# Attention slots taken in pairs once the feed-forward products of the mixer are interleaved with them

## The chip, the cores and the metric

One Trainium2 chip, one NeuronCore. The metric is device time in microseconds (us) of one execution. Before the change it is 1092.57 us, the median of three executions (1092.56, 1092.57 and 1092.97). The profiled execution has a span of 1089.3 us.

## What is computed

Two stages in a row, all in fp32 on 4 batches, 768 positions and 512 channels:

```python
# attention, per batch and head (8 heads of width 64)
scores = where(block_mask, q @ k.T / 8, -1e9)     # blocks of 32: window, first, last, 3 random
x = softmax(scores) @ v                            # heads side by side: (4, 768, 512)
# mixer
u = x + real(fft(fft(x, axis=1), axis=2))
un = (u - mean(u)) / sqrt(var(u) + 1e-6)
out = u + relu(un @ w_ch1) @ w_ch2                 # 512 -> 2048 -> 512
```

## The kernel before

**The unit.** Attention works on pairs of heads (index `n`, 16 in all, four for each batch). A *unit* is one block of 128 keys against 384 queries (half of the 768) for the two heads of a pair. There are 12 units for each head pair: 6 key blocks (`c`) for each of two halves. A unit is made of four pieces:

- `scores` (line 536): the two heads' products k·q, four matrix instructions at line 551. Each head uses 64 rows of the array, so that two run side by side. The result is a PSUM tile `s` of two banks; the pool `ps_s` (line 182) has two of them.
- `weigh` (line 563): ScalarE takes the exponential of `s` in place (line 572), VectorE multiplies it by the mask into an SBUF tile `e` (line 574; the pool `ep`, line 174, has four), and GpSimd adds `e` into a running sum `acc` (line 584). The tile `s` is free when VectorE has read it. (In the first batch the mask is put in by a product, and ScalarE writes `e` itself.)
- `values` (line 587): the two heads' products with v, four matrix instructions at line 597, each head on 64 columns of the array. They accumulate over the 6 key blocks in the single PSUM tile `o` (line 183). After the sixth, `o` is copied out as `oT`, by VectorE (line 604) or ScalarE (line 607), and the next half can write `o`.
- once for each half, `place` or `place_blocks` puts `oT` into the mixer's input `x` (the latter by 16 DMA transfers, line 635), and once for each head pair `total` sums `acc` by TensorE (line 677).

**The mixer.** Its "rest" for a batch is a list of `channel` steps: eight `quad` steps (line 979; seven products of 1.3 us in the plan's figures, a first-layer block with ReLU) and 24 `channels` steps (line 1044; 3.45 us, eight instructions at line 1048, then an add into `x` by VectorE at line 1051). They stand in the order quad, quad, six `channels`, four times. A quad borrows both `s` tiles (line 1009) from its third product on. All that comes ahead of it in the mixer (Fourier sums, normalisation, transposes) is a list of `apart` steps.

**The order.** It is written out by the host when the program is built. `slot(sl)` (line 1271) is called for `sl` = 0 to 96; a slot has two units, six slots make a head pair (`s` = 0 to 5), 24 a batch (`r` = 0 to 23). A slot issues, in this order: the scores of its two units, their `weigh`, the `values` of the *previous* slot's units, loads, then channel steps, then `short` steps (transposes, `place`, `total`). How many channel steps is set by a debt: `state["owed"]` grows by `pace` in each slot and a step is issued as soon as half of it is owed (lines 1332 to 1340). `pace` spreads what is in `late` beyond `COVER` (100 us) over the slots that are left of the batch, and is at least 2.5 us. `gap` (line 1215), called ahead of and after each channel step, slips in `apart` steps that are ready by the host's own estimates.

At two points of a batch (`s` = 5 of its first head pair and `s` = 1 of its second, lines 1298 and 1313) `until` issues all channel steps of the batch two before, since the memory of its `x` is needed. Channels of the first batch are all issued there, so only slots 54 to 96 have any beside them. `BY_VECTOR` = 9: from head pair 9 on, q and k are turned by VectorE (`flip_blocks`, line 514) and put in order by ScalarE (`in_order`, line 523), not by TensorE.

Of the kernel before, what the change touches and what calls it, by code (L numbers as in the profile page):

```python
# [102 lines left out]
def kernel(  # L103
# [16 lines left out]
    B, H, S, D = q.shape  # L120
# [12 lines left out]
    T = C // 2  # L133
# [58 lines left out]
    def busy(engine, us, after=0.0):  # L192
        when[engine] = max(when[engine], after) + us
        return when[engine]
# [13 lines left out]
    pairs = [(b, j) for b in range(B) for j in range(NP)]  # L208
# [325 lines left out]
    SLOT = 2  # L534

    def scores(us):

        n, w = divmod(us[0], UP)
        half = w // C
        qT, kT = turned[n, 0], turned[n, 1]  # L540
        queries = slice(half * HS, (half + 1) * HS)
        got = []
        for u in us:
            c = u % C
            s = ps_s.tile([P, 2, 512], FP32, tag="s", name="s")
            got.append((u, s))
            busy("PE", 0.72, max(e_at.get(u - SLOT, 0.0), z_at[u % 2]))
            s_at[u] = when["PE"] + HOP
            for i in range(2):
                rows = slice(D * i, D * i + D)  # L550
                nc.tensor.matmul(s[:, i, 0:HS], kT[rows, c * P:(c + 1) * P], qT[rows, queries],  # L551
                                 start=True, stop=n >= NP)
        for u, s in got if n < NP else ():
            c = u % C
            busy("PE", 0.25)
            s_at[u] = when["PE"] + HOP
            for i in range(2):
                rows = slice(D * i, D * i + D)
                nc.tensor.matmul(s[:, i, 0:HS], of_k[rows, c * P:(c + 1) * P], off_q[rows, queries],
                                 start=False, stop=True)  # L560
        return got

    def weigh(u, s):
        n, w = divmod(u, UP)
        half, c = divmod(w, C)
        e = ep.tile([P, 2, HS], FP32, tag="e", name="e")
        e_of[u] = e
        if n < NP:
            nc.scalar.activation(out=e, in_=s[:, :, 0:HS], func=ACT.Exp, scale=scale)
            e_at[u] = busy("ACT", 0.8, s_at[u]) + HOP  # L570
            return
        nc.scalar.activation(out=s[:, :, 0:HS], in_=s[:, :, 0:HS], func=ACT.Exp, scale=scale)  # L572
        m = mask[:, c, half * HS:(half + 1) * HS].rearrange("p (o s) -> p o s", o=1)
        nc.vector.tensor_tensor(out=e, in0=s[:, :, 0:HS], in1=m.broadcast_to([P, 2, HS]),  # L574
                                op=ALU.mult)
        e_at[u] = busy("DVE", 0.97, busy("ACT", 0.8, s_at[u]) + HOP) + HOP
        if c > 0:
            acc_at[n, half] = busy("POOL", 2.0, e_at[u]) + HOP
        if c == 1:
            acc_of[n, half] = acc_p.tile([P, 2, HS], FP32, tag="acc", name="acc")  # L580

        for i in range(2 if c > 0 else 0):
            acc = acc_of[n, half][:, i, :]
            nc.gpsimd.tensor_add(out=acc, in0=e_of[u - 1][:, i, :] if c == 1 else acc,  # L584
                                 in1=e[:, i, :])
# [38 lines left out]
    def in_blocks(n):  # L624

        return n > 2 * NP and n % NP > 0
# [20 lines left out]
    def add_up(us):  # L649


        n, w = divmod(us[0], UP)
        half, c = divmod(w, C)
        j = pairs[n][1]
        if c == 0:
            sp_of[n, half] = ps_m.tile([P, 512], FP32, tag="m", name="sp"), bank("m")
        sp, at = sp_of[n, half]
        sp = sp[:, 0:HS]
        busy("PE", 0.85)
        for r, u in enumerate(us):  # L660
            for i in range(2):
                g = BLK * (2 * i + r)
                nc.tensor.matmul(sp[g:g + BLK, :], pick[:, BLK - j:2 * BLK - j], e_of[u][:, i, :],  # L663
                                 start=(c == 0), stop=(c == C - SLOT), tile_position=(0, g))
        if c == C - SLOT:
            into_sums((0, half), j, sp)
            give(at, busy("DVE", 0.6, when["PE"] + HOP))
# [519 lines left out]
    SP = UP // SLOT  # L1187
    SB = SP * NP
    W_PACE = 1.42
    short, apart, late = deque(), deque(), deque()  # L1190
    state = {"w": 0, "got": 0, "owed": 0.0, "ready": 0.0}

    def channel_step():
        late.popleft()[0]()
# [76 lines left out]
    def slot(sl):  # L1271
        phase, r = divmod(sl, SB)
        n, s = divmod(sl, SP)
        units = range(SLOT * sl, SLOT * sl + SLOT)
        if sl < B * SB:
            for u, ps in scores(units):
                weigh(u, ps)
        if not late:
            gap(1.5)
        if 0 < sl <= B * SB:  # L1280
            done = [u - SLOT for u in units]
            for u in done:
                values(u)
            if phase == 0 or sl == SB:
                add_up(done)
            for u in done:
                e_of.pop(u)
        if s == 3 and n + 2 < len(pairs):
            load_q(n + 2)
        if s == 0 and 0 < n < len(pairs) - 1:  # L1290
            load_k(n + 1)

        reuse = n % NP == 0 and phase >= 2
        if sl > 0 and s == (5 if reuse else 3) and sl <= B * SB:
            b, j = pairs[n]
            at = oT_at[n, 0]
            if reuse:
                until(lambda: (b - 2, 0) in finished)
                at = when["PE"] + LEAVES
            if in_blocks(n):  # L1300
                place_blocks(n, 0)
            else:
                short.append(("t", at, lambda: place(n, 0)))
        if 0 < sl <= B * SB and s == 0 and n % NP != 1:
            if in_blocks(n - 1):
                place_blocks(n - 1, 1)
            else:
                short.append(("t", oT_at[n - 1, 1], lambda: place(n - 1, 1)))
        if sl < B * SB and n % NP == 1 and s == 1:
            b = pairs[n - 1][0]  # L1310
            at = oT_at[n - 1, 1]
            if b >= 2:
                until(lambda: (b - 2, 1) in finished)
                at = when["PE"] + LEAVES
            short.append(("t", at, lambda: place(n - 1, 1)))
        if sl > SB and s == 0 and sl <= B * SB:
            short.append(("t", acc_at[n - 1, 1], lambda: total(n - 1)))
        if n + 1 < len(pairs):
            for at, a, half in ((1, 0, 0), (2 if n > 0 else 3, 0, 1), (4, 1, 0), (5, 1, 1)):
                if s == at and n + 1 < BY_VECTOR:  # L1320
                    short.append(("t", 0.0, lambda a=a, half=half: turn(n + 1, a, half)))
            if s == 1:
                load_v(n + 1)
        if sl == 0:
            short.append(("t", 0.0, lambda: turn(0, 1, 1)))
        if sl == 1:
            short.append(("t", 0.0, lambda: turn(0, 0, 1)))
        if phase == 0 and 4 <= sl < 4 + 2 * C:
            short.append(("m", 0.0, lambda: mask_step(sl - 4)))
        if r == 1 and 0 < phase:  # L1330
            begin(phase - 1)
        left = SB * (phase + (0 if r == 0 else 1)) + 1 - sl
        us = sum(step[1] for step in late)
        pace = max(LEAST, min(MOST, (us - COVER) / left)) if left > 0 else MOST
        state["owed"] = min(state["owed"], pace) + pace if late else 0.0
        gap(max(state["owed"], 0.0))
        while late and state["owed"] >= late[0][1] / 2:
            state["owed"] -= late[0][1]
            channel_step()
            gap(max(state["owed"], 0.0))  # L1340

        while short and (s in (2, 5) or len(short) > 1 or phase == 0 or r == 0):
            ready = [i for i in short if max(i[1], min(free[i[0]])) <= when["PE"] + 0.1]
            if not ready and s not in (2, 5) and r > 0 and sl > 1:
                break
            item = ready[0] if ready else short[0]
            short.remove(item)
            item[2]()
        if BY_VECTOR <= n + 1 < len(pairs):
            for at, fn, args in ((0, squares, (n + 1, 0)), (1, flip_blocks, (n + 1, 0)),  # L1350
                                 (2, in_order, (n + 1,)), (4, flip_blocks, (n + 1, 1)),
                                 (5, squares, (n + 1, 1))):
                if s == at:
                    fn(*args)
        w_loads()
        w_steps(sl)
        if sl >= 4 and sl % 2 == 0:
            table_step()
# [140 lines left out]
```

## Time and profile before

| | busy, us | share of the span |
|---|---|---|
| TensorE, products | 1048.1 | 96% |
| TensorE, weight loads | 534.4 | 49% |
| VectorE | 675.3 | 62% |
| ScalarE | 379.1 | 35% |
| GpSimd | 270.2 | 25% |

The share is busy time over the span. The products of TensorE overlap in the records, so 96% is not TensorE at its peak; to see what is lost one compares the distance between two starts with the length of the work itself. By stretches of the trace, the slots that have channels beside them lie at 437 to 590 us and 685 to 815 us:

| stretch, us | what is in it | TensorE | VectorE | ScalarE | GpSimd |
|---|---|---|---|---|---|
| 461 to 590 | slots 56 to 77 with quads and channels | 128.93 | 80.70 | 53.31 | 70.92 |
| 590 to 685 | channels of one batch alone, in `until` | 93.58 | 50.38 | 17.23 | 8.10 |
| 685 to 815 | slots 78 to 95 with quads and channels | 127.10 | 70.76 | 46.34 | 58.89 |
| 815 to 1089.3 | the last values, and the mixers' rests | 263.42 | 153.86 | 42.57 | 5.20 |

### The profile page before, as it was taken

How to read it: one execution, taken by the hardware profiler on the slowest of the kernel's cores; microseconds unless marked ns; L12 is line 12 of the kernel's file. 1: busy time of each engine (PE TensorE's matmuls, PEld its weight loads, DVE VectorE, ACT ScalarE, POOL GpSimd, SP SyncE). 2: the span in 40 equal slices, each digit the busy share in tenths (PEclk: the TensorE clock that was granted, in tenths of full speed). 3: DMA queues.
4: the chain of work that ended last, by engine and by line, in shares of the span. 5: the costliest groups of instructions: out<-in, count | busy, mean ns of one | idle time of the engine just before them, and what ended most of it. 6: DMA issues, size and time to landing. Idle time of an engine off the chain costs nothing.

```text
span 1089.3 us, 12419 instructions
## 1 busy us (share of the span) xinstructions
PE 1048.1 (96%) x4334; PEld 534.4 (49%) x4334; DVE 675.3 (62%) x1241; ACT 379.1 (35%) x762; POOL 270.2 (25%) x302
## 2 busy tenths in 40 slices
PE   8999988988999999999999999999999999999996
PEld 4333333533555545443444555443344555568575
DVE  5899887598745524664567536554556355575663
ACT  6988655555111102353342202334230302220210
POOL 1000186788000001255555000244530001000000
PEclk9999999999999999999999999999999999999999
DMA  7757211121000001222311000212000001000001
GB/s 223 229 163 242 78 45 44 30 45 29 0 1 1 0 1 29 59 38 43 56 22 33 0 1 10 63 37 40 13 8 8 1 1 29 30 1 1 1 17 45
DMA packets 108194, 46.66 MB, mean 43 GB/s; under 512 B 95822, under 2 KB 100956, under 8 KB 108124
## 3 DMA queue, kind: packets, MB, share of 16 engines
q1 hardware_dynamic: 106236, 44.99, 16.2%
q10 hardware_dynamic: 1856, 0.79, 0.3%
q8 instruction: 36, 0.59, 0.2%
q14 instruction: 34, 0.28, 0.1%
q0 software_dynamic: 32, 0.01, 0.0%
HBM read 37.11 MB, written 6.29 MB: 40 GB/s over the span
## 4 chain that ended last, share of the span: by engine, by line
PE 83%; DVE 9%; ACT 3%; issue 2%; DMA 2%; POOL 1%; SPq 0%; ACTq 0%; DVEq 0%; POOLq 0%
PE y L1048 23%; PE z L992 15%; PE s L551 10%; PE o L597 8%; PE yp L992 7%; PE yy L1111 6%; PE xp L992 3%; DVE e L574 3%; PE zp L805 2%; PE sp L663 1%; PE zp L776 1%; DMA out_dram<-x 1%; DVE x L855 1%; POOL acc L584 1%; PE tp L486 1%
## 5 line engine op out<-in xcount | busy, mean ns | idle before, releaser
L584 POOL TENSOR_TENSOR acc<-acc,e 128x384 f32<-128x384 f32 x192 | 196.8, 1058 | 83.8 <-DVE e L574 83.2
L551 PE MATMUL s<-qT,kT 64*128 64x384 f32 x768 | 157.4, 523 | 13.9 <-DVE e L574 12.1
L574 DVE TENSOR_TENSOR e<-s,mask 128x768 f32<-128x768 f32 x144 | 131.1, 948 | 58.6 <-ACT s L572 53.3
L572 ACT ACTIVATE s<-s 128x768 f32<-128x768 f32 x144 | 109.6, 791 | 112.1 <-PE s L551 111.1
L597 PE MATMUL o<-e,vr 128*64 128x384 f32 x768 | 145.5, 500 | 0.0
L1051 DVE TENSOR_TENSOR x<-y,x 128x512 f32<-128x512 f32 x72 | 49.7, 690 | 139.4 <-PE y L1048 139.3
L1048 PE MATMUL y<-w_sb,hA 128*128 128x512 f32 x288 | 129.8, 597 | 1.1 <-ACT zs L807 1.1
L1048 PE MATMUL y<-w_sb,hB 128*128 128x512 f32 x288 | 128.7, 597 | 1.0 <-DVE x L1051 1.0
L551 PEld LDWEIGHTS s<-qT,kT 64*128 64x128 f32 x768 | 63.7, 187 | 89.7 <-DVE e L574 43.1
L584 POOL TENSOR_TENSOR acc<-e 128x384 f32<-128x384 f32 x48 | 49.6, 1055 | 219.6 <-DVE e L574 170.3
L997 DVE TENSOR_TENSOR hA<-z,hA 128x384 f32<-128x384 f32 x64 | 35.7, 557 | 96.3 <-PE z L992 96.3
L992 PE MATMUL z<-unT,t 128*128 128x384 f32 x256 | 93.0, 486 | 0.0
L868 POOL TENSOR_SCALAR st<-st 128x1 f32<-128x1 f32 x24 | 6.6, 276 | 347.0 <-DVE st L867 346.5
L1048 PEld LDWEIGHTS y<-w_sb,hB 128*128 128x128 f32 x288 | 53.3, 190 | 68.5 <-issue 66.5
L1048 PEld LDWEIGHTS y<-w_sb,hA 128*128 128x128 f32 x288 | 52.9, 190 | 64.8 <-issue 58.3
L597 PEld LDWEIGHTS o<-e,vr 128*64 128x64 f32 x768 | 46.8, 137 | 76.3 <-issue 71.1
L1001 ACT ACTIVATE hA<-hA 128x384 f32<-128x384 f32 x64 | 33.5, 523 | 120.1 <-DVE hA L997 119.9
L992 PEld LDWEIGHTS z<-unT,t 128*128 128x128 f32 x256 | 48.6, 190 | 33.9
L1001 ACT ACTIVATE hB<-hB 128x384 f32<-128x384 f32 x64 | 33.5, 523 | 86.3 <-DVE hB L997 86.3
L1012 ACT COPY hA<-xp 128x384 f32<-128x384 f32 x32 | 15.3, 478 | 100.0 <-PE xp L992 100.0
L992 PE MATMUL xp<-unT,w_sb 128*128 128x384 f32 x128 | 48.9, 505 | 1.3 <-DVE x L1051 0.7
L992 PE MATMUL yp<-unT,w_sb 128*128 128x384 f32 x128 | 46.9, 489 | 0.4 <-DVE un L841 0.4
(200 smaller groups left out, 1388.1 us busy)
## 6 DMA issues: line engine op xcount, KB each, us to landing
wraw<-in_moe_w_ch_dram SPq DMA_DIRECT2D x32, 512.0 KB
vr<-in_v_dram SPq DMA_DIRECT2D x30, 192.0 KB
qr<-in_q_dram SPq DMA_DIRECT2D x48, 64.0 KB
x<-oT SPq DMA_DIRECT2D x192, 12.0 KB
kr<-in_k_dram SPq DMA_DIRECT2D x14, 192.0 KB
qb<-in_q_dram SPq DMA_DIRECT2D x28, 96.0 KB
kb<-in_k_dram SPq DMA_DIRECT2D x28, 96.0 KB
out_dram<-x SPq DMA_DIRECT2D x16, 128.0 KB
```

The lines of the kernel that those rows point to most:

```text
L551: nc.tensor.matmul(s[:, i, 0:HS], kT[rows, c * P:(c + 1) * P], qT[rows, queries], start=True, stop=n >= NP)
L572: nc.scalar.activation(out=s[:, :, 0:HS], in_=s[:, :, 0:HS], func=ACT.Exp, scale=scale)
L574: nc.vector.tensor_tensor(out=e, in0=s[:, :, 0:HS], in1=m.broadcast_to([P, 2, HS]), op=ALU.mult)
L584: nc.gpsimd.tensor_add(out=acc, in0=e_of[u - 1][:, i, :] if c == 1 else acc, in1=e[:, i, :])
L597: nc.tensor.matmul(o[D * i:D * i + D, :], vt[:, i, c, :], e[:, i, :], start=(c == 0), stop=(c == C - 1))
L805: nc.tensor.matmul(ps[:, 0:KS - 1], sd[:, t, parts[g - 2]], sn_sb[:, t, :], start=(t == 0), stop=(t == T - 1))
L992: nc.tensor.matmul(to, a[:, k, :], c[:, k, :], start=(k == 0), stop=(k == ND // 2 - 1))
L997: tt(out=to, in0=ps, in1=a, op=ALU.add)
L1001: nc.scalar.activation(out=h, in_=h, func=ACT.Relu)
L1048: nc.tensor.matmul(y, hs[0, half][:, l, m * P:(m + 1) * P], w2_sb[:, 4 * r + l, :], start=(l == 0), stop=(l == 3))
L1051: nc.vector.tensor_tensor(out=x[:, m, :], in0=y, in1=x[:, m, :], op=ALU.add)
L1111: nc.tensor.matmul(ps, a[:, k, :], c[k // 2][:, k % 2, :] if isinstance(c, list) else c[:, k, :], start=(k == 0), stop=(k == 3))
```

## The change

From the first even slot that finds channel steps in `late`, slots go in pairs (`paired`; it stays on). The even slot of a pair `opens` it. It issues its scores, then the values of *both* slots of the pair before, and no channel step, no `apart` step and (but for a batch's first slot) no `short` step. The odd slot issues its scores and then the channel steps that both slots owe. TensorE's order in a pair is so: scores, four units' values, scores, channels. A deque `due` holds the slots whose values are still to come.

Where the older slot in `due` ends a half (its `s` is 2 or 5; since pairs are (0,1), (2,3), (4,5), it is always `s` = 2), its values are issued ahead of the new scores, so that `o` is copied out behind those scores and not in front of the next values. In the other pairs the first of the two slots' values is issued before `weigh` of the new units, since its `e` tiles are the ones that they take over. Some due times of loads, turns and `place` move by one slot so that they fall in odd slots or after the half's last values. The aim is fewer changes of TensorE between its three ways of working (64 rows, 64 columns, whole array) than in two single slots.

```diff
+        opens = sl % 2 == 0
+        state["paired"] |= opens and len(late) > 0
+        paired = state["paired"]
...
-        if sl < B * SB:
-            for u, ps in scores(units):
-                weigh(u, ps)
-        if not late:
-            gap(1.5)
-        if 0 < sl <= B * SB:
-            done = [u - SLOT for u in units]
...
+        if paired and len(due) == 2 and due[0] % SP % T == T - 1:
+            sum_up()
+        got = scores(units) if sl < B * SB else ()
+        if paired and len(due) == 2:
+            sum_up()
+        for u, ps in got:
+            weigh(u, ps)
+        if not paired and not late:
+            gap(1.5)
+        while due and (opens or not paired):
+            sum_up()
+        due.append(sl)
-        if s == 3 and n + 2 < len(pairs):
+        if s == (4 if paired else 3) and n + 2 < len(pairs):
             load_q(n + 2)
...
-        if sl > 0 and s == (5 if reuse else 3) and sl <= B * SB:
+        if sl > 0 and s == (5 if reuse else 4 if paired else 3) and sl <= B * SB:
...
-        gap(max(state["owed"], 0.0))
-        while late and state["owed"] >= late[0][1] / 2:
+        more = paired and opens and sl < B * SB
+        if not more:
+            gap(max(state["owed"], 0.0))
+        while not more and late and state["owed"] >= late[0][1] / 2:
             state["owed"] -= late[0][1]
             channel_step()
             gap(max(state["owed"], 0.0))
 
-        while short and (s in (2, 5) or len(short) > 1 or phase == 0 or r == 0):
+        must = (3, 5) if paired else (2, 5)
+        while short and (not more or r == 0) and (s in must or len(short) > 1 or phase == 0 or r == 0):
```

`sum_up` is new: it takes the oldest slot from `due` and issues the values of its two units, and in the first batch the sums.

More of the change, by code (lines that the diff above doesn't have):

```diff
@@ L1189 @@
     W_PACE = 1.42
-    short, apart, late = deque(), deque(), deque()
-    state = {"w": 0, "got": 0, "owed": 0.0, "ready": 0.0}
+    short, apart, late, due = deque(), deque(), deque(), deque()
+    state = {"paired": False, "w": 0, "got": 0, "owed": 0.0, "ready": 0.0}
     def channel_step():
@@ L1274, in slot, with sum_up @@
         units = range(SLOT * sl, SLOT * sl + SLOT)
-        if sl < B * SB:
-            for u, ps in scores(units):
-                weigh(u, ps)
-        if not late:
-            gap(1.5)
-        if 0 < sl <= B * SB:
-            done = [u - SLOT for u in units]
+        opens = sl % 2 == 0
+        state["paired"] |= opens and len(late) > 0
+        paired = state["paired"]
+        def sum_up():
+            at = due.popleft()
+            done = range(SLOT * at, SLOT * at + SLOT)
             for u in done:
                 values(u)
-            if phase == 0 or sl == SB:
+            if at < SB:
                 add_up(done)
@@ L1318, in slot @@
         if n + 1 < len(pairs):
-            for at, a, half in ((1, 0, 0), (2 if n > 0 else 3, 0, 1), (4, 1, 0), (5, 1, 1)):
+            for at, a, half in ((1, 0, 0), (2 if n > 0 else 3, 0, 1),
+                                (3 if paired else 4, 1, 0), (5, 1, 1)):
                 if s == at and n + 1 < BY_VECTOR:
@@ L1340, in slot @@
             gap(max(state["owed"], 0.0))
-        while short and (s in (2, 5) or len(short) > 1 or phase == 0 or r == 0):
+        must = (3, 5) if paired else (2, 5)
+        while short and (not more or r == 0) and (s in must or len(short) > 1 or phase == 0 or r == 0):
             ready = [i for i in short if max(i[1], min(free[i[0]])) <= when["PE"] + 0.1]
-            if not ready and s not in (2, 5) and r > 0 and sl > 1:
+            if not ready and s not in must and r > 0 and sl > 1:
                 break
```

## The prediction, made before the changed kernel was run

> **What bounds the kernel now.** I read the page first, its chain of work that ended last:
>
> ```profile
> ## 4 chain that ended last, share of the span: by engine, by line
> PE 83%; DVE 9%; ACT 3%; issue 2%; DMA 2%; POOL 1%; SPq 0%; ACTq 0%; DVEq 0%; POOLq 0%
> ```
>
> TensorE carries the chain. So a change pays only by what it takes out of TensorE's own sequence, and costs by what it makes TensorE wait for. Next the timeline of TensorE alone, where slots have channels:
>
> ```profile
> 493.42 1.56 PE L551 MATMUL s<-qT,kT 64*128 64x384 f32 x8
> 494.91 1.51 PE L597 MATMUL o<-e,vr 128*64 128x384 f32 x8
> 496.35 3.70 PE L1048 MATMUL y<-w_sb,hA 128*128 128x512 f32 x8
> 499.99 1.56 PE L551 MATMUL s<-qT,kT 64*128 64x384 f32 x8
> ```
>
> The columns are start, time covered, engine, line. From start to start: scores S 1.49 us, values V 1.44, channel C 3.64, together 6.57. No wait stands in brackets, yet it isn't pure work. Channels alone:
>
> ```profile
> 300.50 10.46 PE L1048 MATMUL y<-w_sb,hB 128*128 128x512 f32 x24
> 310.81 1.46 PE L776 MATMUL zp<-cs_sb,sa 128*128 128x385 f32 x4
> ```
>
> 24 instructions in 10.31 us are 0.43 each, 3.44 for eight. In narrow windows of the same timeline, two side-by-side instructions of S or V follow the last two after 0.32 us, so eight take 1.29. Pure work of a slot is 3.44 + 2 x 1.29 = 6.02. The other 0.55 us lies at the three changes of the array's form: S starts 0.10 late and its second pair comes 0.10 late (C to S 0.20); likewise S to V 0.15 and V to C 0.21. The weight loads, in the whole timeline, show why:
>
> ```profile
> 499.04 0.19 PEld L1048 LDWEIGHTS y<-w_sb,hA 128*128 128x128 f32 x1 [0.24 <-issue]
> 499.98 0.95 PEld L551 LDWEIGHTS s<-qT,kT 64*128 64x128 f32 x8 [0.76 <-issue]
> 499.99 1.56 PE L551 MATMUL s<-qT,kT 64*128 64x384 f32 x8
> ```
>
> Within channels a load comes after 0.24 us of rest, under the running product. At the change it rests 0.76 and starts with its product: it isn't hidden.
>
> Slots with no channel between are bound otherwise:
>
> ```profile
> 464.27 1.78 PE L551 MATMUL s<-qT,kT 64*128 64x384 f32 x8
> 465.98 1.51 PE L597 MATMUL o<-e,vr 128*64 128x384 f32 x8
> 467.47 1.78 PE L551 MATMUL s<-qT,kT 64*128 64x384 f32 x8
> ...
> 717.53 1.86 ACT L528 COPY qT<-qb 128x256 f32<-128x256 f32 x6
> ...
> 721.20 1.78 PE L551 MATMUL s<-qT,kT 64*128 64x384 f32 x8 [1.73 <-DVE e L574]
> ```
>
> S is 0.22 us longer here: its second tile waits for VectorE to read the old one. Of the 42 slots from 54 on nine show this (some 2.0 us), and two have an idle time besides (1.73 and 0.35, 2.1 us). The 1.73 is ScalarE: the six copies of q stand ahead of the exponentials. The chain that frees a tile is read at 499.99:
>
> ```profile
> 500.95 1.50 ACT L572 ACTIVATE s<-s 128x768 f32<-128x768 f32 x2 [3.28 <-PE s L551]
> 501.85 1.82 DVE L574 TENSOR_TENSOR e<-s,mask 128x768 f32<-128x768 f32 x2 [1.06 <-ACT s L572]
> ```
>
> Counted from the start of S the first tile is free at about 2.87 us (501.85 + 0.95, and 0.06 of signal), the second at 3.68.
>
> **What the skill says.** The Trainium skill, "TensorE: Matmul & The Clock Gate", Part 3, "What overlaps and what doesn't", states that a weight load overlaps with running products only where the row group differs, and that products keep strict order. The trace agrees at the changes (0.76 us of rest) but not in general: under channels, whole-array loads do run beneath whole-array products (0.24). So I take the price of a change from the trace alone. "PSUM — Partial Sum Buffer", "Specifications (TRN2)", gives eight banks in each partition; the kernel's pools hold 4 + 1 + 1 + 2 = 8, so no third `s` tile can soften a wait. No run here tests that.
>
> **The change, part by part.** Slots 54 to 95 are 21 pairs: 14 that open at `s` = 0 or 2 (call them A), seven at `s` = 4 (B).
>
> *A, order S VV S C.* Changes: C to S 0.20, S to V 0.15, V to S 0.21 (the same two tenths, read at slots without channels), S to C. The last isn't in this stretch; 1.50 us of S before a whole-array product at 190.97 bounds it to V to C's 0.21, at least 0.15; I take 0.21. Sum 0.77. Before, a pair with channels after both slots pays 2 x (0.20 + 0.15 + 0.21) = 1.12, with channels after one 0.92. Four of the 14 had both: 4 x 0.35 + 10 x 0.15 = 2.9 us saved.
>
> *B, order V S V S C.* Changes 0.20 + 0.21 + 0.15 + 0.21 + 0.21 = 0.98. Three of seven had channels after both: 3 x 0.14 - 4 x 0.06 = 0.2 us. Copying `o` out (VectorE L604, 0.57) lies behind the new scores (1.49). So these gain nothing to speak of.
>
> *Waits that go.* In A four units' values (2.73) stand between the two scores, which then start 4.25 us apart, more than 2.87 and 3.68 ask. Of the nine long S, six are the second of an A pair (1.3 us), and both idle times too, since the copies of q (`s` = 2, an opening slot) fall behind VV: 1.3 + 2.1 = 3.4 us.
>
> *Waits that come.* (1) The `e` ring. The new units' masks write into tiles that V of the pair before has still to read. That V's first unit ends at 1.49 + 0.15 + 0.64 + some 0.15 of signal = 2.45 after S starts, where the mask could have started at 1.86: 0.6 late, so the tile is free at 3.45, the second at 4.35. The second scores need them at 4.25 and 4.99. Price nothing, hidden by VV, but with 0.7 us of slack. Queued behind the waiting mask on VectorE are only `oT` and the next masks, which the next S waits for. (2) S straight after S where a pair has no channel: 2.87 - 1.49 = 1.38 us, less the 0.41 for S to C and C to S that it hasn't, 0.97. By the debt's formula a pair adds twice 2.5 to 3.3; a quad of 9.1 leaves about -3.5, so the pair after owes 1.5 to 2.1, under half of a quad (4.55) or just a channel (1.73). This gives four such pairs; after two of them a B pair follows, whose values of `s` = 2 (1.44) fill the wait. Two stay: 1.9 us. (3) A quad takes the `s` tiles from its third product on, 2.58 us after its start. The second scores' later tile is free 3.68 - 1.49 - 0.21 = 2.0 after it. Hidden, slack 0.6; before, V's 1.44 us lay between too. In B the turn of k (VectorE, 1.52) stands ahead of those masks and takes all of that slack. Price nothing, up to 1 us in each of eight quads. (4) `oT` has one buffer. Sixteen transfers take 10.2 us to issue (the profile's L635), q's loads 2.4 ahead of them; the next copy comes V2, S, V, S, CC, S, V, V later, some 15 us. Free, narrowly. (5) GpSimd adds 3.87 us in a slot, 7.7 in a pair of some 13: hidden. (6) `apart` steps get fewer gaps (none in opening slots), but those of a batch fall largely into the `until` stretches, which stay. Nothing.
>
> All work before slot 54 (to 437 us), in the two `until` stretches and after 815 us keeps its order. Sum: 2.9 + 0.2 + 3.4 - 1.9 = 4.6 us. **Forecast 1092.57 - 4.6 = 1088.0 us.**
>
> **The rivals.** *More:* `total`, `place` and `apart` products fill the gap of S straight after S, and the three long S in B pairs go too: 2.9 + 0.2 + 3.4 + 0.7 = 7.2 us, 1085.4. For it: VectorE is busy only 80.70 of 129 us. Against it: in B two S still lie only 2.9 apart. *Nothing:* the saved waits turn up elsewhere, 3.1 - 2.9 (three waits of 0.97) = +0.2: 1092.4. For it: the masks' chain is as long as before, and it was what ended the waits. *Slower:* `apart` steps come later, `late` is empty longer, so six pairs have no channel to cover them (5.8 us), and eight quads wait 0.6 us each for the tiles (4.8): 10.6 - 6.5 = 4.1 us more, 1096.7. For it: both slacks are 0.6 us, and VectorE may by the host's plan run 2.2 us ahead (`AHEAD`), more than either. Against it: TensorE waits nowhere in 461 to 590 us (128.93 of 129 busy), and quads show no wait for VectorE beyond 0.6 us today.
>
> **From these to numbers.** Forecast 0.48, more 0.14, nothing 0.14, slower 0.24. So faster by over 0.2% (under 1090.4) 0.62, within 0.2% 0.14, slower 0.24. The range has 1085.0 as its low end, which cuts nearly half of "more" (0.06), and 1097.0 as its high end, which cuts half of "slower" (0.12). The unknown prices (S to C 0.15 to 0.21: 1.3 us; quads 0 to 8 us) lie inside.
>
> **What would show it.** Right: in the new timeline a pair reads S 1.49, V of 16 instructions in about 2.73, S 1.50, C; no bracket at the second S; the stretch from 437 to 815 us some 4 to 5 us shorter, all else equal. The wait of L551 for L574 gone from the ends of A pairs, and found only at S straight after S. Wrong: L992 (a quad's `z`) waiting for L574; L574 waiting for L597 so long that S waits in turn; L604 waiting for a transfer; or more than two pairs without a channel.

## The result, and the profile after

| | before | after |
|---|---|---|
| median of four executions, us | 1092.77 (1092.56 to 1095.17) | 1088.67 (1088.13 to 1090.57) |
| ratio, with its 95% interval | | 0.9961 (0.9942 to 0.9979) |
| span of the profiled execution, us | 1089.3 | 1086.9 |
| first S of slot 54 to the sums after the last values, us | 437.06 to 817.07: 380.01 | 438.83 to 814.37: 375.54 |
| what follows, us | 272.23 | 272.53 |

The kernel became 0.39% faster, 4.1 us by the medians. The two profiled executions differ by only 2.4 us, because slot 54 begins 1.77 us later in the one of after. TensorE's order is the same in both up to there, product by product. What differs is the granted clock: ahead of slot 54 it was 0.5 for 3.41 us at four places in the execution of after (one of them at 141 us) and at three in that of before, and 3.41 us at half the clock lose 1.7. So I leave that part out and use the *stretch*: from the first scores of slot 54 to the start of the last sums (line 677). It went down by 4.47 us, where the prediction's sum was 4.6. Whole times agree where the mean granted clock does: in the executions with 0.992 they are 1092.69 to 1093.11 us before (eight of them) and 1088.13 to 1088.77 after (six). All experiments below are compared by the stretch, and by the median.

The chain that ended last, by engine, in the page of after:

```profile
PE 84%; DVE 10%; issue 2%; ACT 2%; POOL 1%; DMA 0%; ACTq 0%; DVEq 0%; POOLq 0%
```

TensorE still carries it. The timeline of TensorE alone, of after (start, time covered, engine, line, and the number of instructions last), shows a pair of each kind:

```profile
493.54 1.56 PE L551 MATMUL s<-qT,kT 64*128 64x384 f32 x8
495.04 2.80 PE L597 MATMUL o<-e,vr 128*64 128x384 f32 x16
497.77 1.56 PE L551 MATMUL s<-qT,kT 64*128 64x384 f32 x8
499.26 7.13 PE L1048 MATMUL y<-w_sb,hA 128*128 128x512 f32 x16
506.32 1.51 PE L597 MATMUL o<-e,vr 128*64 128x384 f32 x8
507.76 1.56 PE L551 MATMUL s<-qT,kT 64*128 64x384 f32 x8
509.25 1.51 PE L597 MATMUL o<-e,vr 128*64 128x384 f32 x8
510.69 1.72 PE L551 MATMUL s<-qT,kT 64*128 64x384 f32 x8
512.35 7.13 PE L1048 MATMUL y<-w_sb,hB 128*128 128x512 f32 x16
```

The first four lines are an A pair, from start to start 1.50, 2.73, 1.49 and 7.06: 12.78 us, where two single slots of before took 13.13. The next five are a B pair, V S V S C: 13.09, no shorter. Its second S takes 1.66 and not 1.49.

What TensorE waits for in the stretch, first in before (line, releaser; us in total, times, longest):

```profile
PE s L551 <- DVE e L574: 2.1, 2, 1.7
PE peak_row L1365 <- DVE peak L1363: 0.8, 1, 0.8
PE xt L619 <- ACT unT L918: 0.7, 1, 0.7
...
PE xp L992 <- DVE x L1051: 0.3, 1, 0.3
```

and in after:

```profile
PE xp L992 <- DVE x L1051: 2.2, 2, 1.8
PE s L551 <- DVE e L574: 1.2, 2, 0.8
...
PE peak_row L1386 <- DVE peak L1384: 0.3, 1, 0.3
```

The waits of scores for the masks fell from 2.1 to 1.2. Quads wait 2.2 us where they waited 0.35, which the prediction didn't have.

The stretch holds the same products in both kernels, only in another order, so the 4.47 us can be split by TensorE's timeline. All waits in brackets together fell by only 0.2 us, from 4.7 to 4.4. The second tile of scores was late by 2.4 us in all before and by 1.95 after, 0.45 less. The places where one product has another form than the one ahead of it (the shape such as 64*128 in its line) went from 133 to 112. What is left of the gain, some 3.8 us, goes with these 21 changes of form, 0.18 each.

By pieces of the stretch (each from a slot's start to another's):

| piece | change, us | what is seen |
|---|---|---|
| slots 54 to 64 | -2.00 | A pairs and a B pair; one slot's values (1.44) moved to the end of the stretch, against 0.5 more of waits in scores and 0.05 in a quad |
| 64 to 66, 70 to 72, 88 to 90, 94 to 96 (B) | -0.39 | -0.03, -0.16, -0.04, -0.16 |
| 66 to 70 | -0.46 | A pairs |
| 72 to 74, and on to `until` | +0.54 | scores straight after scores wait 0.83 |
| 590.7 to slot 84 | -1.48 | 1.73 and 0.68 of waits gone, 1.82 new at 704.17 |
| 84 to 88, 90 to 94 | -1.97 | A pairs; in the last the wait for `peak` fell from 0.82 to 0.30 |
| from 96 on | +1.29 | the values that were moved here |

### The profile page after: what moved, and what is told of

It reads as the page before. It is cut to its first block, busy times and chain, and to the rows that moved or that the text cites. A ratio compares the mean times of both kernels' runs of the same rounds, so it can differ in the third digit from the quotient of the medians.

```text
span 1086.9 us, 12424 instructions
## 1 busy us (share of the span) xinstructions
PE 1046.6 (96%) x4334; PEld 537.4 (49%) x4334; DVE 683.2 (63%) x1241; ACT 380.1 (35%) x762; POOL 271.0 (25%) x302
## 4 chain that ended last, share of the span: by engine, by line
PE 84%; DVE 10%; issue 2%; ACT 2%; POOL 1%; DMA 0%; ACTq 0%; DVEq 0%; POOLq 0%
PE y L1048 22%; PE z L992 15%; PE s L551 10%; PE o L597 9%; PE yp L992 8%; PE yy L1111 6%; PE xp L992 4%; DVE e L574 3%; PE zp L805 2%; PE sp L663 1%; PE zp L776 1%; DVE t L954 1%; PE tp L486 1%; DVE x L855 1%; POOL acc L584 1%
## 5 line engine op out<-in xcount | busy, mean ns | idle before, releaser
L584 POOL TENSOR_TENSOR acc<-acc,e 128x384 f32<-128x384 f32 x192 | 196.3, 1055 | 72.2 <-DVE e L574 71.9
L574 DVE TENSOR_TENSOR e<-s,mask 128x768 f32<-128x768 f32 x144 | 131.2, 949 | 70.3 <-ACT s L572 62.2
L551 PE MATMUL s<-qT,kT 64*128 64x384 f32 x768 | 157.6, 524 | 12.5 <-DVE e L574 10.9
L597 PE MATMUL o<-e,vr 128*64 128x384 f32 x768 | 143.5, 501 | 0.0
L1051 DVE TENSOR_TENSOR x<-y,x 128x512 f32<-128x512 f32 x72 | 49.7, 691 | 125.4 <-PE y L1048 125.2
L584 POOL TENSOR_TENSOR acc<-e 128x384 f32<-128x384 f32 x48 | 51.2, 1088 | 223.2 <-DVE e L574 137.6
L551 PEld LDWEIGHTS s<-qT,kT 64*128 64x128 f32 x768 | 63.8, 187 | 86.7 <-DVE e L574 39.2
L597 PEld LDWEIGHTS o<-e,vr 128*64 128x64 f32 x768 | 48.2, 137 | 75.2 <-issue 72.2
```

What stands on the lines that cost most here:

```text
L597: nc.tensor.matmul(o[D * i:D * i + D, :], vt[:, i, c, :], e[:, i, :], start=(c == 0), stop=(c == C - 1))
L1051: nc.vector.tensor_tensor(out=x[:, m, :], in0=y, in1=x[:, m, :], op=ALU.add)
```

## The experiments

Each row is one kernel; the ratio is to the kernel before, run on the same chip.

| kernel | stretch, us | median, us | ratio (95%) |
|---|---|---|---|
| before | 380.01 | 1092.77 | 1 |
| the change | 375.54 | 1088.67 | 0.9961 (0.9942 to 0.9979) |
| e1, values one slot at a time | 386.37 | 1099.49 | 1.0056 (1.0041 to 1.0072) |
| e2, channels in each slot | 376.59 | 1089.68 | 0.9970 (0.9959 to 0.9981) |
| e3, before with the copies moved | 377.02 | 1090.00 | 0.9971 (0.9962 to 0.9981) |
| e4, sums early | 379.81 | 1092.93 | 0.9996 (0.9985 to 1.0008) |
| e15, sums early, no pair without channels | 373.52 | 1086.85 | 0.9937 (0.9921 to 0.9952) |
| e14, a half's last values early, conditionally | 381.35 | 1095.51 | 1.0019 (1.0010 to 1.0028) |
| e16, e15 and e14 together | 381.06 | 1093.59 | 1.0003 (0.9995 to 1.0011) |
| e5, a half's last values early, always | 385.35 | 1098.08 | 1.0039 (1.0026 to 1.0052) |
| the change, once more | 375.60 | 1088.46 | 0.9957 (0.9943 to 0.9971) |
| e15, once more | 373.60 | 1086.61 | 0.9944 (0.9931 to 0.9957) |

One caution for this table. In the profiled executions of e1, e4, e16 and e5 the granted clock was 0.5 for 3.41 us once within the stretch; in all others it was full there. By the products that ran longer, 1.4 to 1.7 us of each of these four stretches are the clock. Each time TensorE had waited 1.9 to 2.5 us just before; but in e14 it waited 2.52 and the clock stayed full, so no rule follows from this.

**Which half of the change pays?** e1 keeps the grouped channels, and gives up the grouped values (order S V S V C C):

```diff
-        while due and (opens or not paired):
+        while due:
             sum_up()
```

> The channels of two slots stay together in the odd slot and all due times stay as changed, but each slot issues only the values of the slot before it: TensorE's order in a pair is S V S V CC. I measure the stretch from the first S of slot 54 to the first sum (L677) after the last values: 380.0 us before, 375.5 us after the change. Theory (four units' values between two scores do it: they save one form change and, above all, take the wait off the second scores): a pair with two channel steps pays 0.91 us of form changes for 1.12 before, 1.5 us less in about seven pairs, but each second S starts 2.93 us after the first and is some 0.2 us longer, 1.4 us more in the pairs that had a channel between; the ScalarE wait of 1.7 us goes with the channels' move. So 378 to 379 us, 1091 us: most of the gain lost. Rival (moved due times and the q copies standing in another place are all of it): 375.5 to 376.5 us, 1088.7 us.

Measured: 386.37, worse than before by 6.4 us and than either expectation. TensorE's timeline of e1, first from the pair that stands at 493.54 above, then the worst place:

```profile
500.15 1.72 PE L551 MATMUL s<-qT,kT 64*128 64x384 f32 x8
501.81 1.51 PE L597 MATMUL o<-e,vr 128*64 128x384 f32 x8
...
577.01 2.56 PE L551 MATMUL s<-qT,kT 64*128 64x384 f32 x8 [2.02 <-DVE e L574]
```

The sums of e1 over a window at that place (the third figure from the end is the granted clock):

```profile
577.40:580.80 3.40, 3.40 (x12) 1.08 (x10) 1.67 (x3) 2.22 (x5) 3.40 (x4) 0.50 0.14 21
```

The undisturbed pair takes 13.09 (497.22 to 510.31), so the channels' saved change of form, 0.20, is eaten up by a second S of 1.66. The pair's whole gain hangs on VV: 0.15 for the form change and 0.17 because the second S comes late enough. 14 pairs of 0.31 would be 4.3 us of the 10.8 that e1 lies above the change. Another 4.2 us are waits: those of scores for masks are 4.8 us in five places, against 1.2 in after, and that for `peak` 0.9 against 0.3. My reading is that with only 1.44 us between two scores VectorE, once behind, doesn't catch up. Some 1.4 us are the clock: the scores of 577.01 took 2.56 us and the values behind them 2.16, for 1.78 and 1.51 elsewhere. About 0.9 us I can't place. Even without the clock's share grouped channels with single values are worse than no pairs at all.

e2 does the reverse, VV but channels in each slot. `short` steps, `total` among them, may then go in each slot too:

```diff
-        more = paired and opens and sl < B * SB
+        more = False
```

> Four units' values stay together, but each slot issues its own channel steps again, and its short steps too: S VV C S C where two are owed. Theory: V to S is replaced by V to C and C to S, 0.2 us more in the four A pairs that owe channels in both slots (+0.8); in B pairs the extra 0.2 is given back, since the second S isn't long any more. The sum of a head pair (total) falls back into the first slot, so that GpSimd starts its additions earlier and they no longer run beside the four subtractions of VectorE ahead of the batch's first quad: the two waits of that quad (0.40 and 1.82 us) shrink. Stretch 375.5 + 0.8 - 2 = 374 to 376 us, 1088 to 1089 us. Rival (grouping the channels of two slots is the gain): 379 to 380 us, 1092.5 us.

Measured: 376.59, 1.05 above after and just outside the theory's 374 to 376, far from the rival. TensorE's timeline of e2, the same pair:

```profile
492.39 1.56 PE L551 MATMUL s<-qT,kT 64*128 64x384 f32 x8
...
496.61 3.70 PE L1048 MATMUL y<-w_sb,hA 128*128 128x512 f32 x8
500.24 1.56 PE L551 MATMUL s<-qT,kT 64*128 64x384 f32 x8
501.73 3.70 PE L1048 MATMUL y<-w_sb,hA 128*128 128x512 f32 x8
505.36 1.51 PE L597 MATMUL o<-e,vr 128*64 128x384 f32 x8
```

12.97 (492.39 to 505.36): 0.19 more than with grouped channels, as the prediction's list of form changes has it (0.20). The B pair that follows takes 13.13 (505.36 to 518.49) for 13.09, since its second scores aren't long any more. Four A pairs and three B pairs have channels after both slots: 0.9 us. The waits nearly balance. With `total` in the first slot again the quads wait 0.35 and not 2.2, as expected. But a quad stands in an opening slot again (slot 80), and the copies of q behind it, ahead of the exponentials, as before the change. The timeline of e2, all engines:

```profile
717.77 1.86 ACT L528 COPY qT<-qb 128x256 f32<-128x256 f32 x6
...
721.45 1.78 PE L551 MATMUL s<-qT,kT 64*128 64x384 f32 x8 [1.72 <-DVE e L574]
```

So three quarters of the change's gain can be had with the values in pairs alone. That isn't all that grouped channels are worth: e15 below has them and early sums as well, and its stretch is 3.1 us shorter than that of e2.

**Forms or waits?** In e3 the *old* kernel keeps its order of TensorE (but for one transposition in slot 55), and only the turn of k, the squares and the copies of q are issued ahead of the channel steps, where the copies don't stand before the exponentials that scores wait for:

```diff
+        if BY_VECTOR <= n + 1 < len(pairs):
+            for at, fn, args in ((0, squares, (n + 1, 0)), (1, flip_blocks, (n + 1, 0)),
+                                 (2, in_order, (n + 1,)), ...
+                if s == at:
+                    fn(*args)
         left = SB * (phase + (0 if r == 0 else 1)) + 1 - sl
...
-        if BY_VECTOR <= n + 1 < len(pairs):
-            for at, fn, args in (...):
```

> The kernel before, with one thing moved: the q copies, squares and turns of the next head pair (ScalarE and VectorE) are issued ahead of a slot's channel steps, not after them. Theory: the two idle times of TensorE at S (1.73 and 0.35 us), which came from ScalarE work standing ahead of the exponentials after a quad, go, and some 0.2 to 0.4 us of longer S with them: stretch 380.0 - 2.3 = 377.7 us, 1090.4 us, half of the change's gain and no more, since form changes stay. Rival 1 (these waits are all of the gain): 375.5 us, 1088.4 us. Rival 2 (they only move elsewhere): 380 us, 1092.6 us.

Measured: 377.02, 2.99 us less than before. What TensorE waits for in e3 begins with

```profile
PE peak_row L1365 <- DVE peak L1363: 0.8, 1, 0.8
```

No wait of L551 for L574 is left; before had 2.1 us of it. So 3.0 us could be had without any pair. The change takes off both of these waits too, but brings two others of scores (0.32 and 0.83) and gives 1.9 back in quads; it saves form changes besides, which e3 doesn't (133 as before). What it has over e3 in the end is 1.5 us. No run has e3's move and e15's together.

**The new wait of the quads.** The timeline of after, all engines, ahead of the wait:

```profile
697.42 0.85 PE L677 MATMUL sp<-acc,pick 128*32 128x384 f32 x8
698.15 0.69 DVE L954 TENSOR_TENSOR t<-unT 128x512 f32<-128x512 f32 x1
698.38 2.71 POOL L584 TENSOR_TENSOR acc<-e 128x384 f32<-128x384 f32 x2 [12.61 <-PE sp L677]
698.88 1.37 DVE L954 TENSOR_TENSOR t<-unT,t 128x512 f32<-128x512 f32 x1
700.17 1.48 DVE L954 TENSOR_TENSOR unT<-unT 128x512 f32<-128x512 f32 x1
701.06 4.93 POOL L584 TENSOR_TENSOR acc<-acc,e 128x384 f32<-128x384 f32 x4
...
704.17 1.56 PE L992 MATMUL xp<-unT,w_sb 128*128 128x384 f32 x4 [1.82 <-DVE x L1051]
```

`total` (L677) is a `short` step, and now it waits for an odd slot. Until it has read `acc`, GpSimd can't begin the next head pair's sum: it sat idle for 12.61 us. Then its additions come in one heap, just beside VectorE's subtractions of L954. Those take 1.37 to 1.48 us there instead of 0.69, and the L1051 that the batch's first quad waits for stands behind them. GpSimd's waits for L677 in the stretch are 6.8 us in two places in before, and in after

```profile
POOL acc L584 <- PE sp L677: 72.2, 7, 16.0
```

If this chain is right, an earlier `total` takes the wait away. e4 lets `short` steps go in the opening slot of a head pair:

```diff
+        early = paired and s == 0
-        while short and (not more or r == 0) and (s in must or ...):
+        while short and (not more or early) and (s in must or early or ...):
-            if not ready and s not in must and r > 0 and sl > 1:
+            if not ready and s not in must and not early and r > 0 and sl > 1:
```

> The changed kernel, with the sum of a head pair (total, TensorE L677) issued in the opening slot and not in the odd one. It frees acc for GpSimd some 5 to 8 us earlier. Theory: the waits of the batch's first quad for VectorE (0.40 and 1.82 us) come from GpSimd's additions, started late, running beside VectorE's subtractions and making these take 1.4 us for 0.7; they go, -2.2 us. In the last batch the list of channels fills one or two pairs later here, so that S stands straight after S twice in slots 80 to 85, at about 1.0 us each: +1.9 us. Stretch 375.5 - 2.2 + 1.9 = 375.2 us, 1088.4 us; VectorE's L954 on 128x512 back at 0.7 us. Rival (VectorE is late for another reason, its own backlog): L954 stays at 1.4 us, stretch 377.4 us, 1090.6 us.

Measured: 379.81, nearly as slow as before. Some 1.7 us of this are the clock (727.6 to 731.0). The quads' wait did go (0.35 us in all), but scores now wait for masks 4.8 us in four places. TensorE's timeline of e4 in the last batch:

```profile
713.70 1.78 PE L551 MATMUL s<-qT,kT 64*128 64x384 f32 x8 [0.78 <-DVE e L574]
716.77 1.78 PE L551 MATMUL s<-qT,kT 64*128 64x384 f32 x8 [1.29 <-DVE e L574]
...
725.99 1.87 PE L551 MATMUL s<-qT,kT 64*128 64x384 f32 x8 [1.94 <-DVE e L574]
```

These scores come in pairs that have no channel. The batch's `apart` steps came later: L954's last subtraction starts at 726.7 in e4 and at 706.5 in after, the batch's first quad at 733.57 and at 704.17. So e4 by itself doesn't decide. It does show what hangs on the `apart` steps, which the prediction had put at nothing.

e15 is e4, and where `late` is empty with at most six `apart` steps to go, these are issued at once in the odd slot:

```diff
+        if paired and not opens and not late and 0 < len(apart) <= 6:
+            while not late:
+                do_apart()
         left = SB * (phase + (0 if r == 0 else 1)) + 1 - sl
```

> The changed kernel with the sum of a head pair in the opening slot, and the last few steps ahead of a batch's channels (six or fewer) issued at once in an odd slot that finds no channels, so that the first quad comes where it comes in the changed kernel and no pair loses its channels. TensorE's order is that of the changed kernel but for the place of the sums. Theory: GpSimd begins its additions 6 to 8 us earlier and is done when VectorE makes the four subtractions on 128x512 (L954): these take 0.7 us each and not 1.4, the first quad's waits of 0.40 and 1.82 us shrink to 0.35 and nothing or so, and the pair of slots 54 and 55 is 0.9 us shorter as in the run with channels in each slot. Stretch 375.5 - 0.9 - 1.7 = 372.9 us, 1086 us. Rival (the quad waited for VectorE's queue, not for a slow VectorE): 1.8 us of wait stays, stretch 374.6 us, 1087.7 us.

Measured: 373.52, 2.02 us under the change, and 373.60 in its second run. The timeline of e15 at the same place:

```profile
691.28 0.85 PE L677 MATMUL sp<-acc,pick 128*32 128x384 f32 x8
692.24 1.95 POOL L584 TENSOR_TENSOR acc<-e 128x384 f32<-128x384 f32 x2 [7.05 <-PE sp L677]
694.95 3.85 POOL L584 TENSOR_TENSOR acc<-acc,e 128x384 f32<-128x384 f32 x4 [0.77 <-DVE e L574]
699.01 0.68 DVE L954 TENSOR_TENSOR t<-unT 128x512 f32<-128x512 f32 x1
...
700.93 0.69 DVE L954 TENSOR_TENSOR t<-unT,t 128x512 f32<-128x512 f32 x1
```

The sums come six microseconds earlier, GpSimd is done before L954 starts, all four subtractions take 0.68 to 0.69, and the quad waits 0.35 instead of 1.82. In the whole stretch the quads' waits are 0.7 us (2.2 in after), those of scores 0.8 (1.2), and a channel now waits 0.35: 1.5 of the 2.02. TensorE's order is that of after but for the places of the sums, which also leaves two changes of form fewer. One thing moves along: VectorE's copy of the sums (L645, 0.54 us) stood right ahead of that L1051 in after and is gone from there in e15. It is too short for a wait of 1.82, and the three slow subtractions, 2.3 us longer together, are long enough; but no run moves one without the other.

**The one buffer of `oT`.** The prediction called it free, narrowly. e14 sets out to take away the remaining waits, by issuing the last values of a half already in its own opening slot wherever the pair will have a channel step:

```diff
         more = paired and opens and sl < B * SB
+        if more and s == T - 1 and late and min(state["owed"], pace) + pace >= late[0][1] / 2:
+            sum_up()
```

> The changed kernel with the values of the half's last slot (s = 2) issued in that slot, behind the four units' values, wherever a channel step will follow in the odd slot: S V(6 units) S C, and B pairs become S V S C. Five places (slots 62, 68, 74, 86, 92). Theory: a B pair sheds the change from C to V and one of V to S, and pays C to S: 0.2 us less at each place, 1.0 us in all; the mask of the slot's own units is ready at 3.45 and 4.35 us after its scores start, and its values come at 4.2 and 4.9. Stretch 374.5 us, 1087.6 us. Rival (VectorE is late often enough that the third pair of values waits for L574): 0.5 us at each place, stretch 377 us, 1090.2 us.

Measured: 381.35. The gain that was expected came out as a loss of 5.8 us against the change. VectorE's waits in the stretch of e14 have a line

```profile
DVE oT L604 <- DMA x<-oT: 12.8, 4, 3.8
```

and the timelines of VectorE, ScalarE and TensorE show what it does:

```profile
500.36 0.58 DVE L604 STREAM_TRANSPOSE oT<-o 128x384 f32<-128x384 f32 x1 [3.76 <-DMA x<-oT]
...
575.11 0.48 ACT L607 COPY oT<-o 128x384 f32<-128x384 f32 x1 [6.25 <-DMA x<-oT]
...
584.91 1.78 PE L551 MATMUL s<-qT,kT 64*128 64x384 f32 x8 [2.52 <-DVE e L574]
```

The copy out of `o` now comes before the transfers of the half before have read `oT`. The masks (VectorE) and the exponentials (ScalarE) are issued behind the waiting copy, and in the end scores wait for them. So behind the copy at 575.11 come six copies of q (575.48), the exponentials (577.27), and the mask only at 578.16, after 6.74 us of idle time; scores wait 1.71 at 579.17 and 2.52 at 584.91. Scores wait 5.4 us in all against 1.2, and `peak` 1.8 against 0.3: 5.7 of the 5.8 us. A second `oT` would test this more directly; no run has one.

e16 puts e14's edit on top of e15:

> Both edits together: sums early with the forced last steps, and the half's last values early. If the two are separate costs, their gains add: stretch 375.5 - 2.6 - 1.0 = 371.9 us, 1085.0 us. Rival (both draw on the same slack of VectorE): the smaller of the two is lost, 372.9 us, 1086 us.

Measured: 381.06, 7.5 us over e15, with the same waits (scores 5.1 against 0.8, `peak` 1.7 against 0.2) and up to 1.7 us of the clock. e5 issues those values early always, in pairs without a channel too:

```diff
         due.append(sl)
+        if paired and s == T - 1:
+            sum_up()
```

> As the run with the half's last values early, but always, also where no channel follows: then the scores of slots 58 and 82 stand straight after those of 57 and 81, with nothing between. Theory: the price of scores after scores, 2.87 - 1.49 = 1.38 us of wait, less the two form changes saved (0.36) and less the 0.16 by which those scores were long before: 0.9 us each over the changed kernel at these places, 1.8 us in all; the other five places give 1.0 back. Stretch 375.5 + 1.8 - 1.0 = 376.3 us, 1089.4 us, with two waits of about 1.3 us of L551 for L574. Rival (masks keep up, since VectorE has nothing else there): under 0.5 us of wait each, stretch 374 us.

Measured: 385.35, 4.0 us over e14, and far above both expectations, which didn't have the `oT` wait. TensorE's timeline of e5 shows one of two places that it has beyond e14's:

```profile
470.95 1.78 PE L551 MATMUL s<-qT,kT 64*128 64x384 f32 x8 [1.31 <-DVE e L574]
```

The same stands at 729.51. These are scores with nothing between them: they wait 1.31, near the prediction's 1.38. The two make 2.6 of the 4.0 us. The rest is about what the clock took in e5 and not in e14: it was 0.5 from 587.7 to 591.1.

**Once more.** The change and e15 side by side:

> The changed kernel once more, beside the next run and the kernel before. If the 4.5 us of the stretch are all of the change and the rest is chance of an execution, the whole time is 4.5 us below before: ratio 0.9959. If the start of the program (before slot 54) differs by the change too, the ratio is off by the 1.8 us that the two profiles differ there: 0.9943 or 0.9975.

> The version with the sums early and the last steps forced, once more, beside the changed kernel. Its stretch was 373.5 us against 375.5. If that is all, it is 2.0 us (0.2%) below the changed kernel and 6.5 below before: ratio 0.9941 to before. If its first result was luck, it equals the changed kernel: 0.996.

Measured: 0.9957 (0.9943 to 0.9971) and 0.9944 (0.9931 to 0.9957). The intervals of the two ratios overlap. What holds e15 apart from the change are the stretches, 375.54 and 375.60 against 373.52 and 373.60, and medians that lie 1.8 us apart in one and the same session (1088.46, 1086.61).

## Why the prediction was right, point by point

The forecast was 1088.0 us and the time 1088.67; the sum was 4.6 us and the stretch gave 4.47. So close a match is luck in part, since errors cancel. Form changes gave some 3.8 us where 3.1 were forecast. The two idle times of scores went, 2.1 us, and the long scores gave 0.45 more: 2.5 for 3.4. Scores straight after scores cost 0.8 for 1.9, and slot 55 0.3 that wasn't foreseen. Two items were missing from the sum: 1.9 us lost in quads, and 1.2 gained as the waits at `peak` and `xt` shrank (0.5 and 0.7; no run separates why).

- **Form changes in A pairs (2.9).** Right where it can be seen: 0.35 for a pair with channels after both slots, forecast 0.35, and its two parts appear in e2 (channels, 0.19) and in the 2.73 us of VV (0.15). The four changes of an A pair together, with that of scores to a channel taken at 0.21 from a bound, were put at 0.77; they measure 12.78 less 12.04 of pure work (6.88 + 4 x 1.29), 0.74. The count of changes in the list is exact: 21 fewer.
- **B pairs (0.2).** The four B pairs of the table gave 0.39 together, but those of slots 64 and 88, with channels after both slots, only 0.03 and 0.04, forecast 0.14. The term left out that the second S comes 2.9 us after the first, which is too early, so that it takes 0.17 longer.
- **Waits that go (3.4).** Right in kind: both idle times are gone, and e3, which takes away such waits alone, gains 3.0. The count of long scores was misread: five of the nine (slots 57, 61, 69, 73, 85) are the second of an A pair, not six, and the idle time of 1.73 stands at slot 82, which opens a B pair. What took it away is what the prediction named: in after the copies of q run under the VV of slot 80 (716.30), ahead of slot 81's exponentials (718.91). After still has ten long scores, seven of them in B pairs, which the term left out.
- **The `e` ring (0), the tiles of the quads (0).** Right. Masks wait for values in after (L574 for L597, 4.4 us in three places), but the scores next in order (466.60, 691.87 and 717.95) have no bracket and their usual length, and no quad waits for L574.
- **Scores straight after scores (1.9).** The mechanism and its price hold, the count doesn't. Three pairs have no channel (slots 56, 72 and 80), forecast four. After two of them a B pair's values stand between, as forecast. The third waits 0.83 us, with `st` between the scores, and slots 72 to 74 lost 0.46 in all. With nothing between them the wait is 1.31 (e5). "More than two pairs without a channel" had been named as a sign of being wrong; there were three, but the forecast itself counted four, so that sign said nothing.
- **GpSimd (hidden).** This is the step that failed. The prediction asked only whether its 7.7 us of additions fit in a pair, not when they may begin. A postponed `total` holds `acc`, and heaps the additions up beside the subtractions of L954: 1.9 us more of waits in quads.
- **`oT` (free, narrowly).** Right, and e14 and e16 show how narrowly: values moved earlier within one pair made it cost 5.8 us and more.
- **`apart` steps (0).** Right for the change itself. e4 shows that it was no safe zero: later by a few slots, they opened gaps in which scores wait 4.0 us (0.78, 1.29 and 1.94), where the forecast's price of such a place was 0.97.

Of the rivals, "slower" needed six pairs without a channel and a wait in eight quads. Quads did wait, but for another reason, two times and not eight, and 2.2 us in all. "Nothing" needed the masks' chain to bind again; it does so in e1, where VV isn't there, and not in the change.

## What to carry to other kernels

When two kinds of work alternate on a bound engine, grouping can pay twice: by the form changes it saves, and by the distance it puts between two uses of the same buffer. Here the first gave some 3.8 of the 4.5 us, and most of what the second gave was lost again in a wait that the change brought along. Without that distance grouping loses: e1 came out 6.4 us above before, some 1.4 of it the clock. When a step is postponed, don't only ask who waits for its result: ask which buffer it has yet to read, when that lets the next writer begin, and what that writer will then run beside. And before moving work earlier, look for the single buffer that a copy fills: in e14 masks and exponentials were queued behind a copy that waited for it.

## What the runs showed of the hardware

I hadn't expected VectorE to slow down beside GpSimd. A `tensor_tensor` of 128 x 512 elements with both inputs in SBUF (L954) takes 0.68 to 0.69 us alone and 1.37 to 1.48 while GpSimd adds; 128 x 256 takes 0.42 alone and 1.10 beside it. GpSimd's additions suffer as well: 0.97 us each in e15 (1.95 for two), 1.35 in after (2.71 for two). The Trainium skill has this in "SBUF — State Buffer", "Who interferes with whom": a VectorE instruction with two SBUF inputs contends with a GpSimd instruction that reads SBUF, and one with at most one SBUF input doesn't. The trace agrees on both. L1051, whose one input is in PSUM, takes 0.68 us at 703.44 in after, while GpSimd is adding. The page adds that the loser blocks for the whole instruction of the other. The delay here is 0.68 to 0.80 us, somewhat less than one addition of 0.97. That would fit if VectorE came in partway through one, but no run shows it. Read beside L954 and L584, that page turns "GpSimd is hidden" into a question: beside what does it run?
